# The places in SBUF of a three-pass matmul's activation tiles, modulo 256 bytes, one for each chunk

## The chip, the core and the metric

The kernel runs on one core of a Trainium2 chip. The metric is the device time of one execution in microseconds. Three runs of the kernel before took 1074.43, 1074.68 and 1075.53 us; their median is 1074.68 us.

## The reference

Sigmoid attention (8 batches, 12 heads, 448 positions, 64 per head) feeds a gated layer of two products: 3584 tokens, 768 features, 2048 hidden. All in float32:

```python
scores = scale * np.matmul(q, k.transpose(0, 1, 3, 2)) - np.log(S)
attn = 1.0 / (1.0 + np.exp(-scores))
x = np.matmul(attn, v)          # heads side by side: (3584, 768)
h = x @ w_in
relu6 = np.clip(h + 3.0, 0.0, 6.0)
g = h * relu6 / 6.0
return (g @ w_out).astype(np.float32)
```

## The kernel before, in words

**Attention.** For a batch and a pair of heads, TensorE makes scores (lines 210 and 215), ScalarE the sigmoid (222), TensorE the product with the values (236 and 242). These matmuls are fp32 on 64 by 64 quarters of the array; an fp32 matmul of the code stands in the trace as two records.

**The two products by seven.** Each of the two products is cut into 2 by 2 quarters of its operands and done with seven products of quarters instead of eight (Strassen's scheme in Winograd's form, P1 to P7). Sums of weight quarters are made once, by `prep`, and stored in DRAM; sums of activations are made on the core (`t_ops`, `make`).

**Three passes.** A product of quarters keeps float32's precision with operands in fp32r: each operand is split into a high part and a low one, and high x high, high x low, low x high are summed in PSUM (`passes`). Weights are split by `split_w` (lines 290 to 295): a tile `w` of two parts by two pieces of 384 columns, four buffers, used by both products. Activations of the first product are split by `put` (line 257) into a tile `x{k}{c}` for each of the seven products `k` and the three chunks `c` of 128 features, 3584 bytes in each partition. Those of the second product are split by `split_2` (line 418) into tiles `x2` of 7168 bytes, four buffers, each for two of the eight chunks `u` of a quarter's hidden features.

**The first product** (`quads`, matmuls at line 323) takes two row blocks of hidden features at a time. A product of quarters there is 9 matmuls of 128 x 128 weights with 448 activation columns: three passes, and in each pass the three chunks, so that the activation tile changes with every matmul. There are 4 pairs of batches, 4 pairs of row blocks, 7 products, 2 blocks: 224 x 9 matmuls.

**The second product** (`block`, matmuls at line 438, in the last product of all at line 450) has for each of 4 pairs of batches and 7 products the 8 chunks, and for each chunk three passes with three column blocks `e`: again 224 x 9 matmuls. The activation tile stays the same for two chunks, 18 matmuls. Column blocks 0 and 1 go to banks named `y`, block 2 to banks named `yb`.

**The order of the work** is a list of functions, each with a due time in a plan by hand (`at`), sorted once; every engine runs its part of that list in order. The plan counts 0.207 us for a matmul (`TM`).

**The places.** A pool lays its tiles one after the other, in the order in which the program first asks for them; tiles of a pool on the right side lie likewise from the pool's start, which lies the pool's size below the one before. All tiles of concern are whole multiples of 256 bytes, so that every `w` tile starts 64 bytes past a multiple of 256, every `x` and every `x2` tile 128 bytes past one: 64 bytes past the weights. Three tiles that nothing uses set this: `pad3` (line 68) ahead of the first product's pool, `pad4` (line 386) ahead of the second's, and `pad` (line 74). The parts, passes and column slices within these tiles are multiples of 256 bytes as well.

The pool `one` holds the first product's `x`, raw weights `raw`, kept sums `sne` and `snh` and gate results `g`. On its memory the pool `twob` is laid when the first product is done (`close_one`): five of the seven weight tiles of the second product, the gate results of two quarters, and outputs. The pool `twoa`, on the right over attention's memory (`open_two`), holds the `x2` tiles, two weight tiles and the gate results of the other two quarters (`gr`, named g11r and g12r).

Of the kernel before, what the change touches and what calls it, by code (L numbers as in the profile page):

```python
# [8 lines left out]
F32 = mybir.dt.float32  # L9
F32R = mybir.dt.float32r  # L10
# [5 lines left out]
B, H, S, D = 8, 12, 448, 64  # L16
DM, DF = 768, 2048
P = 128
# [16 lines left out]
NW = 7  # L35
# [8 lines left out]
def tile_kernel(ctx: ExitStack, tc: tile.TileContext, qk, vP, w8, outT):  # L44
# [20 lines left out]
    one = ph1.enter_context(tc.tile_pool(name="one", bufs=1))  # L65
    ps = ctx.enter_context(tc.tile_pool(name="ps", bufs=1, space=bass.MemoryType.PSUM))

    one.tile([P, 16], F32, name="pad3")
    bias_s = base.tile([P, 1], F32, name="bias_s")
    nc.gpsimd.memset(bias_s, neg_log_s)  # L70
    bias_3 = base.tile([P, 1], F32, name="bias_3")
# [217 lines left out]
    def split_w(keys, src):  # L289
        w = base.tile([P, 2, 2, W], F32R, tag="w", name=f"w_{'_'.join(map(str, keys[0]))}", bufs=4)  # L290
        h, l = w[:, 0], w[:, 1]
        nc.scalar.copy(h, src)  # L292
        nc.vector.tensor_tensor(out=l, in0=src, in1=h.bitcast(F32), op=ALU.subtract)  # L293
        for i, key in enumerate(keys):
            ring[key] = w[:, :, i]
# [86 lines left out]
    x2, w2, graw, two = {}, {}, {}, {}  # L382

    def open_two():
        ph2.close()
        ctx.enter_context(tc.tile_pool(name="twop", bufs=1, side="right")).tile([P, 16], F32, name="pad4")
        two["a"] = ctx.enter_context(tc.tile_pool(name="twoa", bufs=1, side="right", reuse_waits="tile"))

    def close_one():
        ph1.close()  # L390
        two["b"] = ctx.enter_context(tc.tile_pool(name="twob", bufs=1, reuse_waits="tile"))
# [23 lines left out]

    def split_2(n, k, u):
        split_w([(n, k, u), (n, k, u + 1)], w2[k][:, u : u + 2])
        x = two["a"].tile([P, 2, 2, S], F32R, tag="x2", name=f"x2_{n}_{k}_{u}", bufs=4)
        src = graw[n, held[k]][:, u : u + 2]
        nc.scalar.copy(x[:, 0], src)  # L420
        nc.vector.tensor_tensor(out=x[:, 1], in0=src, in1=x[:, 0].bitcast(F32), op=ALU.subtract)  # L421
        for i in range(2):
            x2[n, k, u + i] = x[:, :, i]

    def block(n, place):
# [56 lines left out]
        for k in range(NW):  # L482
            for u in range(HF):
                if (n, k) != (NT - 1, P4):
                    at(place + k * d + u * TU, unit, k, u)
                if u % 2 == 0:
                    need = place + k * d + u * TU - 6 * TU
                    if n == 0:
                        at(need - 14, load_w2, k, u)
                    if k < 4:  # L490
                        at(need - 15, load_g, n, quarters[k], u)
                    if k in made:
                        at(need - 1.5 if k != P4 else need - 2 * d, make, n, k, u)
                    at(place + k * d + u * TU - 6 * TU + 0.3 - (u == HF - 2), split_2, n, k, u)
# [69 lines left out]
    for j, place in enumerate((  # L564
        marks[0] + 40, marks[1] + 10, marks[1] + 38, marks[1] + 66, starts[2] + 26, starts[2] + 45, marks[2] + 20, marks[2] + 56
    )):
        prep(1, j, place, 12)
    at(marks[3] + 20, open_two)
    at(now + 5.5, close_one)
    first = now  # L570
# [61 lines left out]
```

## Time and profile before

| | |
|---|---|
| median of three runs | 1074.68 us |
| the profiled execution's own time | 1074.61 us |
| its span in the profile | 1072.6 us |
| VectorE busy | 799.4 us |
| ScalarE busy | 628.3 us |
| granted TensorE clock | 1.00 |

The profile calls the engines PE (TensorE's matmuls), PEld (its loads of weights), DVE (VectorE), ACT (ScalarE), POOL (GpSimd) and SP (SyncE, which issues most DMAs). A row of a group names the line of the kernel, the engine, the operation, the tiles written and read, the count, the busy time in us, the mean of one in ns, and the idle time of the engine ahead of them with what ended it. A matmul's duration holds the time that its last column needs through the array, and matmuls overlap: durations don't add up to the time, the distance from start to start does. Attention and the first product take turns up to 665.5 us; the second product follows.

### The profile page before, as it was taken

How to read it: one execution, taken by the hardware profiler on the slowest of the kernel's cores; microseconds unless marked ns; L12 is line 12 of the kernel's file. 1: busy time of each engine (PE TensorE's matmuls, PEld its weight loads, DVE VectorE, ACT ScalarE, POOL GpSimd, SP SyncE). 2: the span in 40 equal slices, each digit the busy share in tenths (PEclk: the TensorE clock that was granted, in tenths of full speed). 3: DMA queues.
4: the chain of work that ended last, by engine and by line, in shares of the span. 5: the costliest groups of instructions: out<-in, count | busy, mean ns of one | idle time of the engine just before them, and what ended most of it. 6: DMA issues, size and time to landing. Idle time of an engine off the chain costs nothing.

```text
span 1072.6 us, 17779 instructions
## 1 busy us (share of the span) xinstructions
PE 1066.3 (99%) x6736; PEld 887.4 (83%) x6736; DVE 799.4 (75%) x1032; ACT 628.3 (59%) x851; POOL 150.6 (14%) x102
## 2 busy tenths in 40 slices
PE   9999999999999999999999999999999999999998
PEld 3447699987999744899849999999999999999998
DVE  4997699776788567787658466877778776967793
ACT  7878845558555578655585455544454455445452
POOL 0523454200033204231200000000000000000000
PEclk9999999999999999999999999999999999999999
DMA  8876999945688647876526871917300730270011
GB/s 284 293 234 229 372 373 308 334 137 163 202 278 296 240 130 242 296 260 208 198 83 202 339 236 69 385 55 258 120 1 9 257 114 1 84 265 30 1 44 61
DMA packets 89653, 206.17 MB, mean 192 GB/s; under 512 B 9952, under 2 KB 53344, under 8 KB 89568
## 3 DMA queue, kind: packets, MB, share of 16 engines
q1 hardware_dynamic: 89424, 204.97, 55.5%
q8 instruction: 53, 0.87, 0.3%
q14 instruction: 32, 0.26, 0.1%
q10 hardware_dynamic: 144, 0.07, 0.0%
HBM read 142.61 MB, written 62.39 MB: 191 GB/s over the span
## 4 chain that ended last, share of the span: by engine, by line
PE 89%; DMA 4%; DVE 3%; issue 2%; POOL 1%; ACT 0%; SPq 0%; ACTq 0%; DVEq 0%; POOLq 0%
PE z L323 33%; PE y L438 24%; PE yb L438 12%; PE sc L215 8%; PE pv L242 8%; DMA raw<-wd 2%; PE pv L236 1%; PE sc L210 1%; PE y L450 1%; DMA w<-wd 1%; DMA wd<-ws 1%; DVE w L293 1%; PE yb L450 0%; POOL ws L158 0%; DVE wa L135 0%
## 5 line engine op out<-in xcount | busy, mean ns | idle before, releaser
L323 PE MATMUL z<-x,w 128*128 128x448 f32 x2016 | 405.1, 362 | 0.8 <-DVE snh L343 0.8
L323 PEld LDWEIGHTS z<-x,w 128*128 128x128 f32 x2016 | 377.7, 188 | 29.5 <-issue 3.5
L438 PE MATMUL y<-x,w 128*128 128x448 f32 x1296 | 366.1, 363 | 0.0
L438 PEld LDWEIGHTS y<-x,w 128*128 128x128 f32 x1296 | 243.4, 188 | 15.5
L438 PE MATMUL yb<-x,w 128*128 128x448 f32 x648 | 233.5, 360 | 0.0
L222 ACT ACTIVATE a<-sc,bias_s 128x896 f32<-128x896 f32 (+1 forms) x172 | 168.5, 991 | 48.7 <-PE sc L215 36.7
L292 ACT CAST w<-w 128x768 fp32r<-128x768 f32 x112 | 93.4, 834 | 167.5 <-PE yb L438 152.4
L293 DVE TENSOR_TENSOR w<-w,w 128x768 fp32r<-128x768 f32 x112 | 107.1, 956 | 90.4 <-ACT w L292 90.1
L293 DVE TENSOR_TENSOR w<-raw,w 128x768 fp32r<-128x768 f32 x112 | 124.2, 1109 | 64.0 <-ACT w L292 58.8
L215 PE MATMUL sc<-qk 64*64 64x448 f32 x1152 | 152.0, 539 | 0.0
L242 PE MATMUL pv<-a,v 64*64 64x448 f32 x1152 | 151.6, 537 | 0.3 <-DVE xr L251 0.3
L438 PEld LDWEIGHTS yb<-x,w 128*128 128x128 f32 x648 | 121.3, 187 | 8.5
L292 ACT CAST w<-raw 128x768 fp32r<-128x768 f32 x112 | 93.2, 832 | 40.0 <-PE z L323 24.1
L149 POOL TENSOR_TENSOR wa<-wa,st 128x768 f32<-128x768 f32 x32 | 65.2, 2038 | 361.1 <-DVE st L145 330.9
L215 PEld LDWEIGHTS sc<-qk 64*64 64x64 f32 x1152 | 58.1, 134 | 54.6 <-issue 36.0
L242 PEld LDWEIGHTS pv<-a,v 64*64 64x64 f32 x1152 | 59.4, 133 | 51.8 <-issue 36.6
L353 ACT ACTIVATE g<-z,bias 128x448 f32<-128x448 f32 x96 | 59.0, 631 | 40.9 <-PE z L323 40.8
L259 DVE TENSOR_TENSOR x<-xr,x 128x448 fp32r<-128x448 f32 x84 | 59.7, 714 | 13.1 <-ACT x L258 11.1
L356 DVE SCALAR_TENSOR_TENSOR g<-g,z 128x448 f32<-128x448 f32 x96 | 57.7, 614 | 15.2 <-ACT g L353 15.2
L251 DVE TENSOR_TENSOR xr<-pv,xr 128x448 f32<-128x448 f32 x48 | 29.7, 619 | 39.3 <-ACT xr L250 39.2
L353 ACT ACTIVATE g<-snh,bias 128x448 f32<-128x448 f32 x32 | 21.5, 671 | 58.1 <-DVE snh L343 52.0
L421 DVE TENSOR_TENSOR x<-g11r,x 128x896 fp32r<-128x896 f32 x48 | 52.1, 1085 | 0.3 <-ACT x L420 0.2
(58 smaller groups left out, 840.0 us busy)
## 6 DMA issues: line engine op xcount, KB each, us to landing
raw<-wd SPq DMA_DIRECT2D x112, 384.0 KB, 4.3
gd_g<-g SPq DMA_DIRECT2D x128, 224.0 KB, 3.7
qk<-qk SPq DMA_DIRECT2D x47, 448.0 KB, 4.9
st<-wi SPq DMA_DIRECT2D x16, 768.0 KB, 6.7
wd<-ws SPq DMA_DIRECT2D x64, 192.0 KB, 5.0
st<-wo SPq DMA_DIRECT2D x16, 768.0 KB, 6.4
v<-vP SPq DMA_DIRECT2D x48, 224.0 KB, 3.3
w<-wd SPq DMA_DIRECT2D x28, 384.0 KB, 7.8
```

Of the source, the lines that this page charges most:

```text
L149: nc.gpsimd.tensor_tensor(out=a, in0=a, in1=e, op=ALU.add)
L215: nc.tensor.matmul(sc[j][halves[h]], k[halves[j], ks], q[halves[j]], start=True, stop=True)
L222: nc.scalar.activation(a[:, j] if len(sc) == 2 else a, x, AF.Sigmoid, bias=bias_s, scale=scale)
L242: nc.tensor.matmul(pv[b, hp][h][halves[j], :S], v[halves[h], j * NC + c], a[halves[h], j], start=c == 0 and not (second and shared), stop= ...
L259: nc.vector.tensor_tensor(out=x[:, 1], in0=xr[q], in1=x[:, 0].bitcast(F32), op=ALU.subtract)
L292: nc.scalar.copy(h, src)
L293: nc.vector.tensor_tensor(out=l, in0=src, in1=h.bitcast(F32), op=ALU.subtract)
L323: nc.tensor.matmul(z[i, k][:, :S], w[:, wu, c * P : (c + 1) * P], X[n, k, c][:, xu], start=m == 0 and k in (P1, P5), stop=m == 3 * HC - 1, ...
L353: nc.scalar.activation(new(i, o), src(i, o), AF.Relu, bias=bias_3, scale=1.0)
L356: nc.vector.scalar_tensor_tensor(out=g[i, o], in0=g[i, o], scalar=6.0, in1=src(i, o), op0=ALU.min, op1=ALU.mult)
L421: nc.vector.tensor_tensor(out=x[:, 1], in0=src, in1=x[:, 0].bitcast(F32), op=ALU.subtract)
L438: nc.tensor.matmul(z[k][e][:, :S], w[:, wu, e * P : (e + 1) * P], x[:, xu], start=u == 0 and i == 0 and k in (P1, P5, P2, P3), stop=u == H ...
```

## The change

The one pad ahead of the pool `one` becomes three, of 32, 64 and 64 bytes, one ahead of each chunk's tiles; for each chunk and product a tile is asked for under the later tag, only to give that tag its place. So the `x` tiles lie chunk by chunk, and those of chunks 0, 1 and 2 start 32, 96 and 160 bytes past the weights modulo 256. In the second product the four buffers under one tag become four tags, one for each pair of chunks, laid first in the pool `twoa`, with pads of 0, 64, 32 and 32 bytes ahead of them and one of 32 behind: -32, 32, 64 and 96 bytes past the weights. The buffers are used in the same turn as before. What follows in these pools moves along: raw weights, kept sums and gate results of the first product from 64 to 160 past the weights, g11r, g12r and the second product's first two weight tiles from 64 to 128. No instruction is added, removed or moved in the order.

```diff
-    one.tile([P, 16], F32, name="pad3")
+    for c, pad in enumerate((8, 16, 16)):
+        one.tile([P, pad], F32, name=f"pad3_{c}")
+        for k in range(NW):
+            one.tile([P, 2, S], F32R, tag=f"x{k}{c}", name=f"place_{k}_{c}")
...
     def open_two():
         ph2.close()
-        ctx.enter_context(tc.tile_pool(name="twop", bufs=1, side="right")).tile([P, 16], F32, name="pad4")
         two["a"] = ctx.enter_context(tc.tile_pool(name="twoa", bufs=1, side="right", reuse_waits="tile"))
+        for i, pad in enumerate((0, 16, 8, 8)):
+            if pad:
+                two["a"].tile([P, pad], F32, name=f"pad4_{i}")
+            two["a"].tile([P, 2, 2, S], F32R, tag=f"x2{i}", name=f"place2_{i}")
+        two["a"].tile([P, 8], F32, name="pad5")
...
     def split_2(n, k, u):
         split_w([(n, k, u), (n, k, u + 1)], w2[k][:, u : u + 2])
-        x = two["a"].tile([P, 2, 2, S], F32R, tag="x2", name=f"x2_{n}_{k}_{u}", bufs=4)
+        x = two["a"].tile([P, 2, 2, S], F32R, tag=f"x2{u // 2}", name=f"x2_{n}_{k}_{u}")
```

## The prediction

> **What bounds the kernel now.** I read the page first (busy times, then the groups), next the waits of TensorE, then the windows of busy time for one line at a time, and last the instructions in order of time over single microseconds.
>
> The page's busy times, and the four waits that TensorE's matmuls have in the whole span:
>
> ```profile
> span 1072.6 us, 17779 instructions
> PE 1066.3 (99%) x6736; PEld 887.4 (83%) x6736; DVE 799.4 (75%) x1032; ACT 628.3 (59%) x851; POOL 150.6 (14%) x102
> ```
>
> ```profile
> PE idle L109 <- DVE idle L76: 1.3, 1, 1.3
> PE z L323 <- DVE snh L343: 0.8, 2, 0.5
> PE pv L236 <- DVE xr L251: 0.4, 1, 0.4
> PE pv L242 <- DVE xr L251: 0.3, 1, 0.3
> ```
>
> TensorE is busy 1066.3 of 1072.6 us and waits for others for 2.8 us in all. No other engine sets the time: it is the number of matmuls times the distance from one matmul's start to the next. The change touches neither the count nor the order, so it can act on that distance alone, and only in the two products, whose operands it moves:
>
> ```profile
> L323 PE MATMUL z<-x,w 128*128 128x448 f32 x2016 | 405.1, 362 | 0.8 <-DVE snh L343 0.8
> L438 PE MATMUL y<-x,w 128*128 128x448 f32 x1296 | 366.1, 363 | 0.0
> L438 PE MATMUL yb<-x,w 128*128 128x448 f32 x648 | 233.5, 360 | 0.0
> ```
>
> That is 2016 in the first product; in the second 1296 + 648, and 72 more from the last column loop (L450): again 2016, so 4032 in all. The mean that a row gives (362 ns) holds the time of the pipeline; the distance comes from windows with one line's instructions (PE busy and count, PEld busy and count, clock, DMA share, GB/s), the first of these three in the first product and the others in the second:
>
> ```profile
> 320.00:360.00 40.00, 40.00 (x201) 37.52 (x201) 1.00 0.88 298
> 860.00:960.00 100.00, 100.00 (x502) 93.81 (x501) 1.00 0.29 99
> 960.00:1050.00 90.00, 90.00 (x452) 84.42 (x451) 1.00 0.12 45
> ```
>
> Counts include those cut at an edge, so 40 us hold 200 matmuls, 100 us hold 500 and 90 us hold 450: 200 ns each, in both products, with the granted clock at 1.00 and whether the DMA engines are 88% or 12% busy. 4032 x 0.200 = 806 us, three quarters of the span. So 1 ns on every one of them is 4.03 us, or 0.38% of the time. About 0.2% (2.1 us, or 0.53 ns a matmul) is what a measurement of this kernel can tell from no change.
>
> **Is there anything to win in 200 ns?** Two readings bear on it. First, in order of time within the second product:
>
> ```profile
> 845.52 0.36 PE L438 MATMUL yb<-x,w 128*128 128x448 f32 x1
> 845.52 0.38 PEld L438 LDWEIGHTS y<-x,w 128*128 128x128 f32 x2
> 845.72 0.56 PE L438 MATMUL y<-x,w 128*128 128x448 f32 x2
> 846.12 0.36 PE L438 MATMUL yb<-x,w 128*128 128x448 f32 x1
> 846.12 0.39 PEld L438 LDWEIGHTS y<-x,w 128*128 128x128 f32 x2
> ```
>
> Three matmuls take 0.60 us (845.52 to 846.12), and a load of weights starts with a matmul: while the activations stream, the weights of a later matmul are read from the same memory. Second, for comparison, the attention products, where a matmul also has 448 columns, but one half of an fp32 product, four side by side in the quarters of the array:
>
> ```profile
> 82.12 0.54 PE L242 MATMUL pv<-a,v 64*64 64x448 f32 x1
> 82.50 0.54 PE L242 MATMUL pv<-a,v 64*64 64x448 f32 x1
> ```
>
> One set of four is 0.38 us after another. If the products' fp32r columns went in at twice that speed, 448 would take 0.19 us; they take 0.20. That is an estimate, since the number format differs, but it is the nearest row: about 10 ns of each matmul aren't explained by its columns.
>
> By the Trainium skill's page "TensorE: Matmul & The Clock Gate" (section "Back-to-back issue gap") the distance would be N/2.4 + 2.5 ns, which for 448 columns is 189 ns; the sum by that floor would be 11 ns x 4032 = 44 us of gain at the most; the windows show 200 ns and so disagree with it.
>
> The instructions of the second product, by least, median and longest duration, say more of these 10 ns:
>
> ```profile
> L438 PEld LDWEIGHTS y<-x,w x1296: 187/188/188, 665.5 to 1053.9; 128*128 128x128 f32 x186
> L438 PE MATMUL y<-x,w x1296: 362/363/364, 665.7 to 1054.1; 128*128 128x448 f32 x186
> L438 PE MATMUL yb<-x,w x648: 359/360/361, 666.1 to 1054.3; 128*128 128x448 f32 x162
> ```
>
> ```profile
> L450 PE MATMUL y<-x,w x48: 359/363/364, 1054.5 to 1063.9; 128*128 128x448 f32 x48
> L450 PE MATMUL yb<-x,w x24: 360/363/364, 1064.1 to 1068.7; 128*128 128x448 f32 x24
> ```
>
> A load never takes other than 187 or 188 ns: nothing delays it. A matmul does vary: every third is 3 ns shorter. At L438 that is always the third column block (bank yb), but at L450, where three matmuls in a row go to one block, both y and yb range from 359 to 364. So the short one belongs to its turn among three, not to a bank. Yet all activations start 64 bytes past the weights modulo 256. So the time isn't one fixed cost: it has a part that passes from one matmul to the next, and a place modulo 256 can act on such a part.
>
> **The change part by part.**
>
> *Product one* (2016 matmuls): chunk 0, 1, 2 of the activations now start 32, 96 and 160 bytes past the weights. The three follow each other within every pass, so all places occur in each run of three, where the pattern of two long and one short now stands. No row shows any place but 64, so the cost is bounded. In favour: all the unexplained 10 ns go, 2016 x 10 = 20 us. Against: as much again is lost, +20 us. Within the rows: the mean of two long and one short is (363 + 363 + 360)/3 = 362; if all were short, 2 ns less, -4.0 us; if all were long, 1 ns more, +2.0 us. I take -4.0 us, since the span of 360 to 363 is the only one that these matmuls show under full load, and a run of three with three places has no reason to settle in the same pattern.
>
> *Product two* (2016 matmuls): the four x2 tiles of a set lie at -32, 32, 64 and 96. One tile serves two chunks, 18 matmuls or 3.6 us, so a place holds for a long time, and the result is the mean of four places, one of them the present one. By the same rows -4.0 us to +2.0 us, and by the wide bounds, on the three quarters that move (1512), 15 us either way. I take -4.0 us, with less confidence than in product one.
>
> *The pads and place tiles* issue nothing: no instruction, no DMA, no wait of their own. They shift other tiles by 96 or 64 bytes: raw, g and the kept sums of product one, the gate's results and two weight tiles of product two. That VectorE or ScalarE would care is spoken against by these rows, where the sources lie at two different places modulo 256 already (g11r at 128, g21r at 64):
>
> ```profile
> L421 DVE TENSOR_TENSOR x<-g11r,x 128x896 fp32r<-128x896 f32 x48 | 52.1, 1085 | 0.3 <-ACT x L420 0.2
> L421 DVE TENSOR_TENSOR x<-g21r,x 128x896 fp32r<-128x896 f32 x32 | 34.7, 1084 | 0.0
> ```
>
> Cost nothing; and if it were some ns, VectorE's 75% would hide it. The order of tiles in memory changes too: product two's later pool lies over other tiles of product one than before. The first loads into it go out well after product one's end at 665.5 us:
>
> ```profile
> 670.32 0.38 SPq L397 DMA_DIRECT2D w<-wd  x1
> 670.80 0.88 SPq L404 DMA_DIRECT2D g22r<-gd_g  x2
> ```
>
> All activations are free by then, so no load waits longer on the DMA queue, and none behind it.
>
> *What is late next:* if matmuls become 1% faster, raw weights must come 1% faster. In the first window above the DMA engines are 88% busy; early in product one they are full:
>
> ```profile
> 140.00:150.00 10.00, 10.00 (x52) 9.38 (x51) 1.00 1.01 361
> ```
>
> There the gain may be lost, but that group lasts 34 us (133 to 167), so at most 0.3 us. The sum: -4.0 - 4.0 = -8.0 us. The profiled execution took 1074.61 us, its span and 2.0 us around it, 0.07 us under the median of 1074.68; 1074.61 - 8.0 = 1066.6 us.
>
> **The rivals.**
>
> *No change.* The weights of a load cover 512 bytes and the activations of a matmul 1792: two and seven whole rounds of 256. If the two reads disturb each other wherever their places meet, whole rounds meet equally often from any start, and the 10 ns stay; so they do if they are a fixed cost of fp32r. For it: 200 ns in windows of such different DMA load. Against: the turn of three. It gives 1074.6 us. The same follows if the tiles don't land where the change means them to.
> By the Trainium skill's page "TensorE: Matmul & The Clock Gate" (section "Step-by-step: what each phase is for") loads and activations have read ports of their own and don't take bandwidth from each other, so by that rule too no place could matter; the turn of three neither proves nor refutes it.
>
> *Slower: 64 is a good place.* If the reads meet, a matmul may lose by its start: at 64 the activations would run ahead of the weights, and elsewhere catch up with them and stand still. The moved matmuls are 2016 + 1512 = 3528; with half of the present 10 ns again for each, 5 ns x 3528 = +17.6 us, 1092.3 us; with 1 ns, +3.5 us. It decides as soon as the moved ones take over 200.6 ns in the mean. For it: both products have the same 64, and nothing in the trace says that other places are better. Against: nothing either; no other place is there to compare.
>
> *Much faster.* The places keep the reads apart and nearly all of the 10 ns go: -40 us, 1034.6 us; with half, 1054.6 us. For it: the comparison with attention. Against: product two keeps one place for 18 matmuls, so every one of the four would have to be good.
>
> **How the numbers follow.** Forecast 0.32 (its own range 1058 to 1072), much faster 0.10, no change 0.30, slower 0.28, half of that within 14 us. So faster 0.42, same 0.30, slower 0.28. The range of 1050 to 1088 leaves out the larger part of the much faster case and the dearer third of the slower one, not quite 2 in 10.
>
> **What would show it.** The windows of L323 and L438: 100 us should hold 505 matmuls where now 500. The durations of L323 and L438 should lose the 363 against 360, or have it in other turns. In product two I look at each x2 tile's own matmuls: 18 in a row at one distance, then 18 at another, would show that the place decides; the same 200 ns at all four would show the no-change rival. Wrong would be a time set elsewhere: waits of TensorE above 3 us, or loads (PEld) longer than 188 ns.

## The result: slower by 1.5%

The changed kernel takes 1091.35 us (median of four runs, 1090.14 to 1092.21), against 1075.11 us of the kernel before beside it (1074.43 to 1075.54): a ratio of 1.0148, 95% interval 1.0133 to 1.0163. Its profiled span is 1088.1 us, 15.5 us longer. The page's first lines, TensorE's waits and the matmul groups of the changed kernel, whose lines have moved down by 3 to 7:

```profile
span 1088.1 us, 17778 instructions
PE 1082.5 (99%) x6736; PEld 874.8 (80%) x6736; DVE 800.5 (74%) x1032; ACT 629.8 (58%) x851; POOL 148.5 (14%) x102
```

```profile
PE idle L112 <- DVE idle L79: 1.3, 1, 1.3
PE pv L239 <- DVE xr L254: 0.4, 1, 0.4
PE pv L245 <- DVE xr L254: 0.3, 1, 0.3
```

```profile
L326 PE MATMUL z<-x,w 128*128 128x448 f32 x2016 | 413.4, 367 | 0.0
L445 PE MATMUL y<-x,w 128*128 128x448 f32 x1296 | 369.0, 366 | 0.0
L445 PE MATMUL yb<-x,w 128*128 128x448 f32 x648 | 237.1, 366 | 0.0
```

TensorE's busy time grew by 16.2 us (1066.3 to 1082.5), its waits fell from 2.8 to 2.0 us, VectorE's and ScalarE's busy times grew by 1 to 2 us. So it is the distance from one matmul's start to the next that grew. Windows in the first and in the second product (PE busy and count, PEld, DVE, ACT, POOL, clock, DMA share, GB/s):

```profile
450.00:530.00 80.00, 80.00 (x393) 73.45 (x392) 63.75 (x85) 42.36 (x66) 18.82 (x12) 1.00 0.70 225
700.00:800.00 100.00, 100.00 (x493) 92.09 (x492) 74.44 (x82) 50.58 (x65) 0.00 (x0) 1.00 0.38 136
```

80 us hold some 392 matmuls where before 400, and 100 us some 491 where before 500. From the starts of all matmuls in the trace the mean is 204.43 ns in the first product and 203.80 in the second. 2016 x 4.43 + 2016 x 3.80 = 16.6 us; about 1 us of waits and short stops in the first product fell away, which leaves the 15.5 us by which the span grew.

In the second product each tile's 18 matmuls can be read off. In order of time, every third matmul (`yb`) of three tiles in turn, at places 32, 64 and 96:

```profile
825.00 0.37 PE L445 MATMUL yb<-x,w 128*128 128x448 f32 x1
...
827.49 0.37 PE L445 MATMUL yb<-x,w 128*128 128x448 f32 x1
...
828.09 0.36 PE L445 MATMUL yb<-x,w 128*128 128x448 f32 x1
...
831.09 0.36 PE L445 MATMUL yb<-x,w 128*128 128x448 f32 x1
...
832.32 0.37 PE L445 MATMUL yb<-x,w 128*128 128x448 f32 x1
...
834.78 0.36 PE L445 MATMUL yb<-x,w 128*128 128x448 f32 x1
```

Twelve matmuls at place 32 take 2.49 us, 15 at place 64 take 3.00, 12 at place 96 take 2.46. Over all 504 matmuls of each place the mean is 206.8 ns at 32, 200.0 at 64, 205.0 at 96 and 203.4 at -32. The one place of four that the kernel had before has kept its time to 0.01 ns. Each place is met 27 times before the last product of all, and at one place the means of the single tiles differ by at most 0.24 ns.

### The profile page after: what moved, and what is told of

Same layout as the page of the kernel before. It is cut to its first block, busy times and chain, and to the rows that moved or that the text cites. A ratio compares the mean times of both kernels' runs of the same rounds, so it can differ in the third digit from the quotient of the medians.

```text
span 1088.1 us, 17778 instructions
## 1 busy us (share of the span) xinstructions
PE 1082.5 (99%) x6736; PEld 874.8 (80%) x6736; DVE 800.5 (74%) x1032; ACT 629.8 (58%) x851; POOL 148.5 (14%) x102
## 4 chain that ended last, share of the span: by engine, by line
PE 97%; DVE 2%; issue 1%; DMA 0%; SPq 0%; ACT 0%; DVEq 0%; ACTq 0%
PE z L326 38%; PE y L445 24%; PE yb L445 12%; PE sc L218 9%; PE pv L245 9%; PE pv L239 2%; PE sc L213 1%; PE y L457 1%; PE yb L457 0%; DVE xr L266 0%; DVE xr L254 0%; DMA wd<-ws 0%; PE idle L112 0%; DVE wa L142 0%; DVE x L262 0%
## 5 line engine op out<-in xcount | busy, mean ns | idle before, releaser
L326 PE MATMUL z<-x,w 128*128 128x448 f32 x2016 | 413.4, 367 | 0.0
L445 PE MATMUL yb<-x,w 128*128 128x448 f32 x648 | 237.1, 366 | 0.0
L218 PE MATMUL sc<-qk 64*64 64x448 f32 x1152 | 147.3, 539 | 0.1
L245 PE MATMUL pv<-a,v 64*64 64x448 f32 x1152 | 146.8, 536 | 0.3 <-DVE xr L254 0.3
L218 PEld LDWEIGHTS sc<-qk 64*64 64x64 f32 x1152 | 53.0, 134 | 60.0 <-issue 43.9
L245 PEld LDWEIGHTS pv<-a,v 64*64 64x64 f32 x1152 | 53.6, 133 | 57.7 <-issue 47.1
```

The costliest lines, as they stand in the source:

```text
L218: nc.tensor.matmul(sc[j][halves[h]], k[halves[j], ks], q[halves[j]], start=True, stop=True)
L245: nc.tensor.matmul(pv[b, hp][h][halves[j], :S], v[halves[h], j * NC + c], a[halves[h], j], start=c == 0 and not (second and shared), stop= ...
L326: nc.tensor.matmul(z[i, k][:, :S], w[:, wu, c * P : (c + 1) * P], X[n, k, c][:, xu], start=m == 0 and k in (P1, P5), stop=m == 3 * HC - 1, ...
L445: nc.tensor.matmul(z[k][e][:, :S], w[:, wu, e * P : (e + 1) * P], x[:, xu], start=u == 0 and i == 0 and k in (P1, P5, P2, P3), stop=u == H ...
```

## The experiments

The theory going in: the place of a matmul's activations past the weights sets its distance, and 64 is the best of the four. The rivals: absolute addresses, the change of place from one matmul to the next, or the tiles that moved along.

**Each half alone, the map, and the weights moved.** Where no more runs are named, a kernel was run once, and its distances are those of one execution. The first two kernels take one half of the diff each. The third lays one place for each product of quarters in the first product, and 128, 160, 192 and 0 in the second:

```diff
+    for k, pad in enumerate((0, 8, 8, 8, 8, 8, 8)):
+        if pad:
+            one.tile([P, pad], F32, name=f"pad3_{k}")
+        for c in range(HC):
+            one.tile([P, 2, S], F32R, tag=f"x{k}{c}", name=f"place_{k}_{c}")
...
-        for i, pad in enumerate((0, 16, 8, 8)):
+        for i, pad in enumerate((0, 8, 8, 16)):
```

The fourth is the kernel before with one number changed:

```diff
-    base.tile([P, 8], F32, name="pad")
+    base.tile([P, 16], F32, name="pad")
```

> The places of the first product alone (32, 96, 160); the second product as before, all at 64. Theory (the place of a matmul's activations past the weights sets its distance from the next one): the first product keeps the 204.4 ns a matmul that it has in the changed kernel, the second goes back to 200.0: 1075 + 2016 x 4.4 ns = about 1084 us. Rival (the two products hinder each other, or the tiles that moved along cost something): not the sum of parts, e.g. 1075 or 1091 us.

> The places of the second product alone (-32, 32, 64, 96); the first as before. Theory: the first product at 200.0 ns, the second at 203.8 as in the changed kernel, with 206.7 at place 32, 200.0 at 64, 205 at 96 and 203.4 at -32: 1075 + 2016 x 3.8 ns = about 1082.5 us. Rival: as for the run with the first product alone; the two gains over before would not add up to the 16.2 us of the change.

> Each of the first product's seven products of quarters has one place for its three chunks: 0, 32, 64, 96, 128, 160, 192 past the weights, in the order P1, P5, P6, P2, P7, P3, P4; the second product's four tiles lie at 128, 160, 192 and 0. Theory (the place decides): in the first product 206.7 ns at 32, 200.0 at 64, about 205 at 96, as the second product has them in the changed kernel, though the activation tile changes with each matmul; 0, 128, 160 and 192 between 200 and 210, the same in both products. Rival (the change of place from one matmul to the next costs): all seven at about 200 ns in the first product, since no place changes within a run of three. Rival of the forecast (all places meet equally often): refuted by the changed kernel already, and again if the seven differ.

> The idle pad ahead of the weight tiles is 32 bytes longer, so weights and the first product's activations both start 32 bytes later (place 64 kept) and the second product's activations stay where they were, which makes their place 32. Theory (the distance between activations and weights modulo 256 decides): first product 200.0 ns, second 206.7 ns at every tile: 1075 + 2016 x 6.7 ns = about 1088 us. Rival (the activations' own address modulo 256 decides): first product changes from 200.0, second stays at 200.0 ns.

Measured, with 1074.78 us for the kernel before: 1082.67 and 1083.93 us for the halves, with 204.43 and 200.0 ns in the one, 200.0 and 203.80 in the other. The losses against before (7.9 and 9.2 us) add up to the change's 16.2 within 1 us; the second run's start of the first product, which lies between 133.2 and 135.2 us from profile to profile, is enough for the rest (133.2 in the profile before, 134.8 here). The map (1084.78 us) gave in the first product 202.7, 205.9, 200.0, 205.0, 204.1, 200.0 and 202.1 ns for 0, 32, 64, 96, 128, 160 and 192, and in the second 202.5, 203.6, 200.2 and 202.1 for 0, 128, 160 and 192. So a place gives about the same in either product, and constant places aren't all at 200: the cost needs no change of place from one matmul to the next. The fourth kernel took 1088.57 us; its windows:

```profile
450.00:530.00 80.00, 80.00 (x402) 75.00 (x401) 63.82 (x85) 43.43 (x70) 18.80 (x12) 1.00 0.69 220
700.00:800.00 100.00, 100.00 (x486) 90.97 (x485) 74.13 (x82) 48.37 (x60) 0.00 (x0) 1.00 0.31 108
```

Where both operands moved, 200.0 ns stayed; where the weights alone moved, the second product's distance rose to 206.7 ns (485 in 100 us). The relation of the two counts, not the activations' address.

**Finer places, and which load.** The fifth kernel reaches places off the 32-byte grid by an offset inside larger tiles; the sixth starts the low part of each weight tile 32 bytes later (to make room, the warm-up matmuls ahead of all work get 80 columns in place of 336):

```diff
-        w = base.tile([P, 2, 2, W], F32R, tag="w", name=f"w_{'_'.join(map(str, keys[0]))}", bufs=4)
-        h, l = w[:, 0], w[:, 1]
+        w = base.tile([P, 4 * W + 64], F32R, tag="w", name=f"w_{'_'.join(map(str, keys[0]))}", bufs=4)
+        h, l = (w[:, o : o + 2 * W].rearrange("p (i n) -> p i n", i=2) for o in (0, 2 * W + 8))
```

> Places off the 32-byte grid, by offsets within the tiles: in the first product 16, 48, 80, 112, 144, 176 and 208 past the weights for P1, P5, P6, P2, P7, P3, P4 (one tile per product of quarters instead of three); in the second product 56, 72, 152 and 168. Theory A (only the 32-byte step counts that a tile starts in): the distance of the step below, as the map run has it: 16 like 0 (202.6 ns), 48 and 56 like 32 (206), 72 and 80 like 64 (200.0), 112 like 96 (205), 144 and 152 like 128 (204), 168 and 176 like 160 (200), 208 like 192 (202). Theory B (the place counts byte by byte): other values, some outside 200 to 206.7, and then perhaps one under 200.

> The low part of each weight tile starts 32 bytes later; activations are at 64 past the high part and so at 32 past the low part. Of nine matmuls, numbers 0 to 5 use high weights, 6 to 8 low ones; the load that runs beside number n is that of n + 1. Theory (what counts is the load that runs beside the matmul): numbers 5, 6 and 7 near 206 ns, the others near 200. Rival (what counts is the matmul's own weights): numbers 6, 7 and 8 near 206 ns. Both give a mean near 202 ns, 1084 us. (Warm-up matmuls are shorter: 80 columns.)

Fine places (1094.07 us): 201.1, 202.9, 203.0, 206.6, 206.1, 203.8 and 204.1 ns for 16 to 208 in the first product; 205.1, 206.4, 206.4 and 204.5 for 56, 72, 152 and 168. 72, just past 64, has 206.4, where the 32-byte step alone would give 200.0. So the bytes count, as theory B has it, but none has a mean under 200. With the low weights moved (1081.83 us) the nine matmuls, numbered 0 to 8, have 197.5, 201.7, 200.8, 197.5, 201.7, 202.5, 205.0, 205.9 and 200.8 ns. Against the turn of three ahead of them, numbers 5, 6 and 7 are 1.7, 7.5 and 4.2 ns longer and number 8 is not, though its own weights are low ones. In the trace the load of the next matmul starts 2 to 4 ns after a matmul's start, and it is this load, running beside a matmul, that fits, not the matmul's own weights. The mean, 201.5, is under the 202 expected.

**Fewer columns, shorter loads.** Two kernels compute only 320 or 384 of 448 columns of the second product, two others only 64 or 32 of 128 output rows, each at the changed kernel's places in the second product and place 64 in the first. The first line that comes in below is that of the kernel with 320 columns, the second that of the kernel with 64 rows (`D`); splits and stores are limited to the same size:

```diff
-                        z[k][e][:, :S], w[:, wu, e * P : (e + 1) * P], x[:, xu],
+                        z[k][e][:, :320], w[:, wu, e * P : (e + 1) * P], x[:, xu, :320],
...
+                        z[k][e][:D, :S], w[:, wu, e * P : e * P + D], x[:, xu],
```

> In the second product only the first 320 of 448 columns are computed, split and stored (the rest is left out), at the changed kernel's places -32, 32, 64, 96. Theory (the excess comes from the reads of a load of 128 columns, which stays): every distance falls by 128 columns at full speed, 53.3 ns: 150.1, 153.4, 146.7 and 151.7 ns. Rival (the excess is a share of the columns streamed): times 320/448: 145.3, 147.7, 142.9 and 146.4 ns. Wrong reading possible if VectorE, with less time for the splits, becomes the bound: then TensorE shows waits.

> As the run with 320 columns, with 384 (the other 64 of 448 are left out in the second product); places -32, 32, 64, 96. With 320 columns all four places had 146.7 ns, 13.3 over the columns at full speed. Theory A (a fixed 13.3 ns, and a part by place that appears only where the columns outlast the load by enough): 173.3 ns at place 64, and the other three between 173.3 and the full part by place, that is up to 176.8, 180.0 and 178.3 ns. Theory B (the part by place needs all 448 columns): 173.3 ns at all four. Rival (a share of the columns): 171.4 ns at place 64.

> In the second product a load has 64 columns of weights instead of 128, so that only 64 of 128 output rows are computed and stored (the other half is left out); places as in the changed kernel. Theory (the excess over 186.7 ns, 448 columns at full speed, comes from the reads of the load beside a matmul): with half the reads about half the excess at each place: -32 195, 32 197, 64 193.3, 96 196 ns. Rival (the excess belongs to the columns or to the format, whatever the load): 203.4, 206.7, 200.0 and 205 ns, as in the changed kernel.

> As the run with loads of 64 columns, with 32 (32 of 128 output rows are computed and stored in the second product). With 64 the distances were 200.2, 204.7, 201.7 and 203.9 ns at -32, 32, 64, 96: the floor of 200 stayed and the mean above it fell from 3.8 to 2.6 ns. Theory A (a floor of 200 ns that no load makes, and a part above it that the load's reads make): all between 200 and 203, mean above the floor under 2 ns. Theory B (the loads make the floor too): some place under 199 ns. Rival (the load has no part in it): 203.4, 206.7, 200.0, 205.

With 320 columns (968.12 us) all four places had 146.6 to 146.9 ns, with 384 (1024.19 us) -32 and 64 had 173.5, 32 had 176.7 and 96 had 176.4. A window of the kernel with 320 columns:

```profile
700.00:800.00 100.00, 100.00 (x684) 100.00 (x683) 88.48 (x122) 58.56 (x86) 0.00 (x0) 1.00 0.39 138
```

The floors 200.0, 173.5 and 146.7 ns (the least means) fall by (200.0 - 146.7)/128 = 0.416 ns a column; 448 columns are 186.6 ns, and 13.4 ns remain. The third length agrees: 384 columns are 159.9 ns, and 13.6 remain. The share-of-columns rival is out, and so is a part by place that stays whole with fewer columns. The loads of the two short-load kernels (1081.08 and 1079.84 us), by least, median and longest duration in ns:

```profile
L442 PEld LDWEIGHTS y<-x,w x1296: 133/134/139, 666.4 to 1060.1; 128*64 128x64 f32 x186
```

```profile
L442 PEld LDWEIGHTS y<-x,w x1296: 106/108/109, 665.6 to 1059.4; 128*32 128x32 f32 x186
```

The loads did get shorter (188 to 134 to 108 ns), but the distances didn't follow: at -32, 32, 64 and 96 they were 200.2, 204.7, 201.7, 203.9 with half loads and 203.4, 202.0, 205.7, 200.0 with quarter loads; means of 202.7 and 202.8. No theory or rival on record for these two kernels gave all four values. With shorter loads other places were good. The floor stayed at 200.0, and the mean above it went from 3.8 to 2.7 ns with half loads and no further (2.8) with quarter loads. My theory of a cost in proportion to the load's reads fell here.

**Sequences, and one place for all.** What was left was that a matmul passes something on to the next. The next kernels are the kernel before with other pads: 64, 160, 64 for the chunks and 160 in the second product; 32 everywhere; the same again, run ten times; 160 everywhere. The edit for 32:

```diff
-    one.tile([P, 16], F32, name="pad3")
+    one.tile([P, 8], F32, name="pad3")
...
-        ctx.enter_context(tc.tile_pool(name="twop", bufs=1, side="right")).tile([P, 16], F32, name="pad4")
+        ctx.enter_context(tc.tile_pool(name="twop", bufs=1, side="right")).tile([P, 24], F32, name="pad4")
```

> Only places that gave 200.0 ns when they stood alone: in the first product 64, 160, 64 for the three chunks, in the second 160 for all tiles. Theory (the place of each matmul alone sets its distance): 200.0 ns in both products, the time of before, about 1075 us. Rival (the sequence counts too, as a disturbed matmul passes something on to the next): the second product at 200.0, the first above it, as the changed kernel's first product has 204.4 ns where the map's values of its three places have a mean of 203.6; 1 ns there is 2 us.

> Both products as before, with one place for all activations, but 32 past the weights instead of 64 (two pads of 32 and 96 bytes in place of 64 and 64). Theory (place decides, and parts add): 206.7 ns in both, 1075 + 4032 x 6.67 ns = 1102 us, less about 1 us of waits in the first product that fall away. Rival (the first product is less sensitive, since its activation tile changes at each matmul): under 1097 us.

> The same kernel as the run with all activations at 32 (1096.68 us, of which 738 matmuls of the first product at 200.0 ns and not 206.7). Theory (each stop of TensorE chooses one of two rhythms, 200.0 or 206.7 ns, kept to the next stop): in the profile whole stretches between stops at the one or the other, not the same stretches as before; times spread over some us, between 1075 (all at 200.0) and 1102 (all at 206.7). Rival (the stretch at 200.0 belongs to that part of the program): the same stretch again, times within 1 us of 1096.7.

> All activations at 160 past the weights. Theory (160 has a rhythm of 200.0 ns, as 64 has, and no slower one): 200.0 ns in both products, the same time as before, 1075 us within 0.2%. Rival (160 has a slower rhythm too, and met the good one by chance where it was tried): stretches between stops at more than 200 ns, 1078 us or more.

Two good places mixed (1079.82 us) gave 202.6 ns in the first product: 202.2 in a turn of nine (197, 203, 203, 201, 204, 202, 203, 206, 201) up to a stop of TensorE at 617.5 us, and 204.4 from there to its end at 671 us, in another turn (201, 208, 205, 200, 209, 204, 201, 208, 204). A stop is here a distance of over 240 ns from one start to the next. A window behind that stop:

```profile
622.00:668.00 46.00, 46.00 (x227) 42.28 (x226) 26.25 (x37) 23.39 (x37) 0.00 (x0) 1.00 0.46 155
```

The 202.2 alone don't show that the sequence counts: two matmuls at 200.0 and one at 206.7, which place 160 turned out to have too, have the same mean. The 204.4 at the same places in the same execution is what no fixed distance for each place gives. All at 32 (1096.68 us) missed its 1102, for the first product had 206.7 ns up to 375 us, exactly 200.0 between 439 and 618 us, and 206.7 again after two stops of TensorE at 618 and 620 us. Its windows, then those of the same kernel's second profile:

```profile
290.00:360.00 70.00, 70.00 (x341) 63.67 (x340) 57.61 (x77) 39.26 (x61) 22.88 (x15) 1.00 0.83 280
450.00:530.00 80.00, 80.00 (x401) 75.08 (x401) 65.75 (x87) 44.40 (x70) 18.79 (x12) 1.00 0.72 232
700.00:800.00 100.00, 100.00 (x485) 90.98 (x484) 73.44 (x81) 49.66 (x63) 0.00 (x0) 1.00 0.39 139
```

```profile
290.00:360.00 70.00, 70.00 (x341) 63.67 (x340) 58.25 (x79) 39.46 (x61) 22.89 (x15) 1.00 0.83 276
450.00:530.00 80.00, 80.00 (x402) 75.08 (x401) 65.64 (x88) 43.37 (x68) 18.82 (x12) 1.00 0.72 233
700.00:800.00 100.00, 100.00 (x502) 93.88 (x501) 76.03 (x84) 51.29 (x65) 0.00 (x0) 1.00 0.37 128
```

The same program, the same places, on two chips, both at a granted clock of 1.00: the second product ran at 206.7 ns (484 in 100 us) in one execution and at 200.0 (500) in the other. A third rhythm, 204.4 ns (206.7 in the first profile), stands in the second profile between two stops at 159 and 237 us. The other stretches came out alike in both profiles: 206.7 ns from 270 to 374 us, 200.0 from 438 to 617. So the stretch at 200.0 did come again, as the rival had it, while the times did not stay within 1 us: ten runs of this kernel on one chip took from 1080.17 to 1100.45 us (median 1093.70), each at a granted clock of 1.00. All at 160 did likewise, so the theory that 160 has no slower rhythm fell: 1079.43 to 1093.88 us in four runs, with this profile, at 206.7 ns in the first and third window and at 200.0 in the second:

```profile
290.00:360.00 70.00, 70.00 (x341) 63.33 (x340) 58.84 (x79) 39.44 (x62) 24.56 (x16) 1.00 0.83 277
450.00:530.00 80.00, 80.00 (x402) 75.10 (x401) 64.39 (x86) 43.36 (x68) 18.76 (x12) 1.00 0.72 228
700.00:800.00 100.00, 100.00 (x486) 90.48 (x485) 73.43 (x81) 49.64 (x63) 0.00 (x0) 1.00 0.36 128
```

Thirteen runs of the kernel before beside these lay between 1074.56 and 1076.84 us, and wherever 64 was the one place of a product with full loads and 448 columns, every stretch of over a hundred matmuls between stops had a mean of 200.00 to 200.06 ns, in eight executions. So a place doesn't set a distance: it sets which rhythms TensorE can fall into. In these profiles the rhythm changed only at a stop and was kept up to the next. What picks it there isn't known; it isn't chance alone, since the stretches from 270 to 374 us and from 438 to 617 us had the same rhythms in all three profiles with 32 or 160 for all activations. At 32 and at 160 there are rhythms of 200.0 and 206.7 ns; at 64 only one of 200.0 was seen. In these three profiles and in the first products of the changed kernel and of the mix of 64 and 160, the means settle on 200.00, 202.22, 204.44 or 206.67 ns: nine matmuls take 1.80, 1.82, 1.84 or 1.86 us. A change of tile, as in the second product of the changed kernel, seems to act as such a start: each place meets the same rhythm each time (means within 0.24 ns), and that kernel's four runs spread by only 2.1 us. What in the memory or the array makes these rhythms wasn't found.

## Why the prediction was wrong

The forecast was 1066.6 us, 8 us less than before; the kernel takes 16 us more.

**The bound** was right: the distance between matmuls alone changed, and no other engine took over. VectorE and ScalarE were busy 1.1 and 1.5 us longer, with moved tiles, and cost TensorE nothing: its waits fell, and none of them is for a DMA.

**The step that failed** is the one for product one, and with it that for product two: "I take -4.0 us, since the span of 360 to 363 is the only one that these matmuls show under full load". The short matmul of three isn't a state that all can have. It is one beat of a rhythm whose mean, 200.0 ns, is the least that any place, sequence or load length gave with 448 columns; singles down to 195 ns stand beside others of 212 (place 128). In place of -4.0 and -4.0 us the terms measured +8.9 and +7.7 us. That the time isn't one fixed cost and passes something on from matmul to matmul was read rightly from the same rows; that a change of it could only be a gain was not in them. (Loads vary a little more than the prediction says, 186 to 192 ns in the first product; nothing rests on that.)

**The 10 ns** that the columns didn't explain are 13.4 ns, nearly the same at 320, 384 and 448 columns, and no place tried had less, so nothing was won; the much faster rival fell with that. The Trainium skill's "TensorE: Matmul & The Clock Gate" (section "Back-to-back issue gap") has 2.5 ns there, for a gap that it calls isolated, with no budget for loads. The runs, with a load for every matmul, have 13.4 ns, and the measurement decides.

**The rival of no change** fell, since a place does matter. The same page of the Trainium skill (section "Step-by-step: what each phase is for") has the loads on a read port of their own that takes nothing from the running matmul; here a move of the weights alone took the second product from 200.0 to 206.7 ns, so in this kernel the two aren't independent. That run is one execution, and place 32 also has a rhythm of 200.0 ns; what stands against chance is that place 64 alone, with full loads and 448 columns, never showed 206.7 in eight executions.

**The slower rival** ("64 is a good place") gave 1092.3 us, 1 us from the result. Its price, half of 10 ns on 3528 moved matmuls, was nearly right by luck of size: 16.6 us / 3528 = 4.7 ns. Its mechanism, activations that catch up with the weights, isn't shown: with half or a quarter of the words read the places changed roles. Where it said that nothing spoke for or against it, the profile had a hint: 200 ns in every window of both products, through all the turns with attention. None of the three profiles with 32 or 160 for all activations has that.

## What to carry to other kernels

Where TensorE is the bound, take the distance from start to start over hundreds of matmuls, not the duration of one, and look at it stretch by stretch between stops: a kernel can run at 200 ns in one stretch and at 206.7 in the next with the same code. The place of the activations against the weights modulo 256 bytes is worth up to 2% here (1096.68 us in the profiled run with all at 32, against 1075.59); a place is only good if repeated runs and every stretch show the same distance, and one run of a place is one draw among its rhythms. The fixed 13 ns a matmul weren't won back by any place; fewer and longer matmuls would pay them less often, which wasn't tried.

## What the runs showed of the hardware that was not expected

An fp32r matmul of 128 x 128 weights costs 0.416 ns a column and 13.4 ns besides, at the least mean over hundreds of matmuls, when the next load runs beside it. The same program at the same addresses has several stable rhythms of matmuls (200.0, 204.4 and 206.7 ns at place 32), changed only at a stop of TensorE and kept for up to 2276 matmuls; its time varied by 20 us, from 1080 to 1100. Loads of 64 and 32 columns of weights take 134 and 108 ns where 128 take 188, and none of them changes the least distance, 200.0 ns.
